# A decode kernel's w_up split between all partitions and the lower 64, and its output row stored by one engine

## The chip, the cores and the metric

The kernel runs on one core of one Trainium2 chip. The metric is the device time of one execution in microseconds (us), the median of several runs. A profile of one execution gives the trace; its span, from the program's first instruction to its last, is a little shorter than the device time.

## What is computed

One token is decoded by two branches that a scalar gate mixes. Branch A is attention of 32 query heads over the last 4096 positions of 8 key/value heads; branch B is a gated linear unit. The change touches only how `B_w_up` is loaded and multiplied and how the 512 outputs are stored.

```python
# x: 1x1x512, wq: 512x4096, caches: 1x8x65536x128, wo: 4096x512
# w_gate, w_up: 512x1792, w_down: 1792x512, gate_w: 512, all bf16
def reference(A_x, A_k_cache, A_v_cache, A_wq, A_wo, B_x, B_w_gate, B_w_up, B_w_down, gate_w):
    x = A_x
    g = sigmoid((x * gate_w).sum(-1, keepdims=True))
    q = x @ A_wq                                   # 32 heads of 128
    k, v = last 4096 positions of the caches       # each used by 4 query heads
    a = softmax(q @ k.T * 128**-0.5) @ v @ A_wo
    b = (sigmoid(x @ B_w_gate) * (x @ B_w_up)) @ B_w_down
    return g * a + (1 - g) * b                     # 1x1x512
```

## The kernel before

The work is mostly loading: 30.67 MB of weights and cache pass through once. SyncE issues the loads in this order: `wq_sb`, four `kn` (K), `wg_sb` (w_gate), `wu_sb` and two `wx_sb` (w_up), four `vv` (V), two `wo_sb`, four `wd_sb` (w_down). ScalarE loads only `x` and `gate_w`. `P` is 128, `D` 512, `DC` 4, `F` 1792, `FQ` 448 and `NJ` 14.

w_up stands in two tiles. Its first 384 rows lie in `wu_sb`, three rows to each of 128 partitions. Its last 128 rows lie in `wx_sb`, two rows to each of partitions 0 to 63, loaded 32 partitions at a time:

```python
    wg_sb = w14.tile([P, DC, F], BF16, name="wg_sb", tag="w14")
    dq.dma_start(wg_sb[:], B_w_gate.rearrange("(p c) f -> p c f", c=DC))
    wu_sb = w14.tile([P, DC, F], BF16, name="wu_sb", tag="w14")


    UC = DC - 1
    UR = UC * P
    dq.dma_start(wu_sb[:, 0:UC, :], B_w_up[0:UR, :].rearrange("(p c) f -> p c f", c=UC))
    wx_sb = const.tile([64, 2, F], BF16, name="wx_sb")
    wx_v = B_w_up[UR:D, :].rearrange("(b j i r) f -> b i j (r f)", b=2, j=4, i=8)
    for b in range(2):
        dq.dma_start(wx_sb[32 * b:32 * b + 32, :, :].rearrange("p r f -> p (r f)"), wx_v[b])
    # ...
    vv = []
    for a in range(HP):
        vv.append(blk.tile([P, NP, P], BF16, name="vv", tag="blk"))
        load_pair(vv[a], A_v_cache, a)
```

`vv` uses the same four buffers as `kn` (pool `blk`), so each `vv` load waits until VectorE has transposed the K tile before it.

The token `x` is turned into columns to match those layouts: four columns for rows `4p+c`, three for rows `3p+c`, and two columns of 64 for `wx_sb`:

```python
    xt_ps = ps_m.tile([P, DC + UC], F32, name="xt_ps", tag="m")
    for c in range(DC):
        nc.tensor.matmul(xt_ps[:, c:c + 1], lhsT=xr[:, 0, c:D:DC], rhs=ident[0:1, 0:1],
                         start=True, stop=True, skip_group_check=True)
    for c in range(UC):
        nc.tensor.matmul(xt_ps[:, DC + c:DC + c + 1], lhsT=xr[:, 0, c:UR:UC], rhs=ident[0:1, 0:1],
                         start=True, stop=True, skip_group_check=True)
    xx_ps = ps_m.tile([64, 2], F32, name="xx_ps", tag="m")
    xp = const.tile([1, 2, 64], BF16, name="xp")
    for r in range(2):
        nc.vector.tensor_copy(xp[:, r, :].rearrange("o (b i j) -> o b i j", b=2, j=4),
                              xr[:, 0, UR:D].rearrange("o (b j i r) -> o b i j r", b=2, j=4, i=8)[:, :, :, :, r])
        nc.tensor.matmul(xx_ps[:, r:r + 1], lhsT=xp[:, r, :], rhs=ident[0:1, 0:1],
                         start=True, stop=True, skip_group_check=True)
    xT = const.tile([P, DC + UC], BF16, name="xT")
    nc.vector.tensor_copy(xT[:], xt_ps[:])
    xx = const.tile([64, 2], BF16, name="xx")
    nc.vector.tensor_copy(xx[:], xx_ps[:])
```

The products of w_gate and w_up go to one PSUM tile each, four blocks of 448 columns on four groups of 32 partitions. `glu(1, ...)` stands after the attention product and takes (3 + 2) x 4 = 20 matmuls:

```python
    def glu(w, parts):
        for n, (x_c, w_c) in enumerate(parts):
            for j in range(4):
                nc.tensor.matmul(gu_ps[w][32 * j:32 * j + 32, 0:FQ], lhsT=x_c.to_broadcast([x_c.shape[0], 32]),
                                 rhs=w_c[:, j * FQ:(j + 1) * FQ], start=(n == 0), stop=(n == len(parts) - 1))
    # ...
    glu(1, [(xT[:, DC + c:DC + c + 1], wu_sb[:, c, :]) for c in range(UC)]
        + [(xx[:, r:r + 1], wx_sb[:, r, :]) for r in range(2)])
```

The end sums both branches in PSUM, the two halves of the row on partitions 0 and 32, then copies and stores each half. SyncE stores what VectorE copied, ScalarE what it copied itself:

```python
    for c in range(NC_O):
        add_row(oY[:, c:c + 1], wo_sb[:, c, :], c == 0, False)
    for j in range(NJ):
        add_row(hT[:, j, 0:1], wd_sb[:, j, :], False, j == NJ - 1)
    res = work.tile([P, HN], BF16, name="res")
    nc.vector.tensor_copy(res[0:1, :], a_ps[0:1, 0, 0:HN])
    nc.sync.dma_start(out[0, :, 0:HN], res[0:1, :])
    nc.scalar.copy(res[32:33, :], a_ps[32:33, 1, 0:HN])
    nc.scalar.dma_start(out[0, :, HN:N_OUT], res[32:33, :])
```

Of the kernel before, what the change touches and what calls it, by code (L numbers as in the profile page):

```python
# [12 lines left out]
BF16 = mybir.dt.bfloat16  # L13
F32 = mybir.dt.float32
# [3 lines left out]
def kernel(  # L18
# [14 lines left out]
    nc = tc.nc  # L33

    P = 128
    D = A_x.shape[-1]
    DC = D // P
# [8 lines left out]
    F = B_w_gate.shape[1]  # L46
    NJ = F // P
    N_OUT = A_wo.shape[1]
    NC_O = HQ * DH // P
    FQ = F // 4  # L50
# [11 lines left out]
    const = ctx.enter_context(tc.tile_pool(name="const", bufs=1))  # L62
# [4 lines left out]
    work = ctx.enter_context(tc.tile_pool(name="work", bufs=1))  # L67
    ps_big = ctx.enter_context(tc.tile_pool(name="ps_big", bufs=2, space=bass.MemoryType.PSUM))
    ps_S = ctx.enter_context(tc.tile_pool(name="ps_S", bufs=2, space=bass.MemoryType.PSUM))
    ps_m = ctx.enter_context(tc.tile_pool(name="ps_m", bufs=2, space=bass.MemoryType.PSUM))  # L70


    xr = const.tile([1, 2, D], BF16, name="xr")
# [3 lines left out]
    dq = nc.sync  # L77
# [15 lines left out]
    wg_sb = w14.tile([P, DC, F], BF16, name="wg_sb", tag="w14")  # L93
    dq.dma_start(wg_sb[:], B_w_gate.rearrange("(p c) f -> p c f", c=DC))
    wu_sb = w14.tile([P, DC, F], BF16, name="wu_sb", tag="w14")


    UC = DC - 1
    UR = UC * P
    dq.dma_start(wu_sb[:, 0:UC, :], B_w_up[0:UR, :].rearrange("(p c) f -> p c f", c=UC))  # L100
    wx_sb = const.tile([64, 2, F], BF16, name="wx_sb")
    wx_v = B_w_up[UR:D, :].rearrange("(b j i r) f -> b i j (r f)", b=2, j=4, i=8)
    for b in range(2):
        dq.dma_start(wx_sb[32 * b:32 * b + 32, :, :].rearrange("p r f -> p (r f)"), wx_v[b])

    vv = []
    for a in range(HP):
# [16 lines left out]
    ident = const.tile([P, P], BF16, name="ident")  # L124
# [17 lines left out]
    nc.vector.tensor_reduce(selI[:], identf[:].rearrange("p (x r) -> p r x", x=4), axis=AX.X, op=ALU.add)  # L142


    xt_ps = ps_m.tile([P, DC + UC], F32, name="xt_ps", tag="m")
    for c in range(DC):
        nc.tensor.matmul(xt_ps[:, c:c + 1], lhsT=xr[:, 0, c:D:DC], rhs=ident[0:1, 0:1],  # L147
                         start=True, stop=True, skip_group_check=True)
    for c in range(UC):
        nc.tensor.matmul(xt_ps[:, DC + c:DC + c + 1], lhsT=xr[:, 0, c:UR:UC], rhs=ident[0:1, 0:1],  # L150
                         start=True, stop=True, skip_group_check=True)
    xx_ps = ps_m.tile([64, 2], F32, name="xx_ps", tag="m")
    xp = const.tile([1, 2, 64], BF16, name="xp")
    for r in range(2):
        nc.vector.tensor_copy(xp[:, r, :].rearrange("o (b i j) -> o b i j", b=2, j=4),
                              xr[:, 0, UR:D].rearrange("o (b j i r) -> o b i j r", b=2, j=4, i=8)[:, :, :, :, r])
        nc.tensor.matmul(xx_ps[:, r:r + 1], lhsT=xp[:, r, :], rhs=ident[0:1, 0:1],
                         start=True, stop=True, skip_group_check=True)
    xT = const.tile([P, DC + UC], BF16, name="xT")
    nc.vector.tensor_copy(xT[:], xt_ps[:])  # L160
    xx = const.tile([64, 2], BF16, name="xx")
    nc.vector.tensor_copy(xx[:], xx_ps[:])
# [20 lines left out]
    for u in range(4):  # L183
        nc.tensor.matmul(S_ps[u // 2][:, u % 2, :], lhsT=other[:].rearrange("p o y u -> p (o y u)"),  # L184
                         rhs=ident[0:2, 0:2].rearrange("p (o y) -> p o y", o=1).to_broadcast([2, 256, 2]),
                         start=True, stop=False)
# [11 lines left out]
    for k in range(8):  # L198
        q_ps = ps_big.tile([P, 512], F32, name="q_ps", tag="b")
        ks = slice(k * 512, (k + 1) * 512)  # L200
        for c in range(DC):
            nc.tensor.matmul(q_ps[:], lhsT=xT[:, c:c + 1].to_broadcast([P, P]),  # L202
                             rhs=wq_sb[:, c, ks], start=(c == 0), stop=(c == DC - 1))
# [18 lines left out]
    for a in range(HP):  # L222
        for v in range(2):
            kT = kTs[a, v] if (a, v) in kTs else k_transpose(a, v)
            k_v = kT[:].rearrange("p (n dhi s t) -> p n dhi s t", n=KB, dhi=2, s=32)
            for dhi in range(2):
                for t in range(2):
                    for hb in range(2):
                        nc.tensor.matmul(S_ps[v][:, hb, :], lhsT=q_st[:, a, dhi, :, t],  # L229
                                         rhs=k_v[:, hb * 16:(hb + 1) * 16, dhi, :, t],  # L230
                                         start=False, stop=(a == HP - 1 and dhi == 1 and t == 1))


    gu_ps = [ps_big.tile([P, 512], F32, name="gu_ps", tag="b") for _ in range(2)]

    def glu(w, parts):
        for n, (x_c, w_c) in enumerate(parts):
            for j in range(4):
                nc.tensor.matmul(gu_ps[w][32 * j:32 * j + 32, 0:FQ], lhsT=x_c.to_broadcast([x_c.shape[0], 32]),  # L239
                                 rhs=w_c[:, j * FQ:(j + 1) * FQ], start=(n == 0), stop=(n == len(parts) - 1))  # L240


    pm2 = work.tile([P, 2], F32, name="pm2")
    for v in range(2):
        nc.vector.tensor_reduce(pm2[:, v:v + 1], S_ps[v][:].rearrange("p a b -> p (a b)"), axis=AX.X, op=ALU.max)  # L245
    pm = work.tile([P, 1], F32, name="pm")
    nc.vector.tensor_tensor(pm[:], pm2[:, 0:1], pm2[:, 1:2], op=ALU.max)
    glu(0, [(xT[:, c:c + 1], wg_sb[:, c, :]) for c in range(DC)])
    sge = work.tile([P, FQ], F32, name="sge")
    nc.scalar.activation(sge[:], gu_ps[0][:, 0:FQ], AF.Exp, scale=-1.0)  # L250
    mt_ps = ps_m.tile([1, P], F32, name="mt_ps", tag="m")
# [6 lines left out]
                     start=True, stop=True)  # L258
# [21 lines left out]
    HN = N_OUT // 2  # L280
    pv_ps = ps_S.tile([P, 4, P], F32, name="pv_ps", tag="S")
    a_ps = ps_S.tile([P, 2, 512], F32, name="a_ps", tag="S")

    def add_row(lhsT, rhs, start, stop):
        for i in range(2):
            nc.tensor.matmul(a_ps[32 * i:32 * i + 1, i, 0:HN], lhsT=lhsT, rhs=rhs[:, i * HN:(i + 1) * HN],  # L286
                             start=start, stop=stop)
# [5 lines left out]
    for a in range(HP):  # L293
        for m in range(NP // 4):
            nc.tensor.matmul(pv_ps[32 * a:32 * a + 32, :, :],  # L295
                             lhsT=eT[:, a, 4 * m:4 * m + 4, :].rearrange("p n r -> p (n r)"),
                             rhs=vv[a][:, 4 * m:4 * m + 4, :],
                             start=(m == 0), stop=(m == NP // 4 - 1))
# [6 lines left out]
    nc.scalar.copy(pv_sb[:], pv_ps[:])  # L305


    glu(1, [(xT[:, DC + c:DC + c + 1], wu_sb[:, c, :]) for c in range(UC)]
        + [(xx[:, r:r + 1], wx_sb[:, r, :]) for r in range(2)])

    o_ps = ps_m.tile([P, HQ], F32, name="o_ps", tag="m")
    for n in range(4):
# [21 lines left out]
        add_row(oY[:, c:c + 1], wo_sb[:, c, :], c == 0, False)  # L334
    for j in range(NJ):
        add_row(hT[:, j, 0:1], wd_sb[:, j, :], False, j == NJ - 1)
    res = work.tile([P, HN], BF16, name="res")
    nc.vector.tensor_copy(res[0:1, :], a_ps[0:1, 0, 0:HN])  # L338
    nc.sync.dma_start(out[0, :, 0:HN], res[0:1, :])
    nc.scalar.copy(res[32:33, :], a_ps[32:33, 1, 0:HN])  # L340
    nc.scalar.dma_start(out[0, :, HN:N_OUT], res[32:33, :])


# [28 lines left out]
```

## Time and profile before

| What | Value |
|---|---|
| Device time, median of 3 runs | 80.81 us (80.67 to 80.82) |
| Span of the profiled execution | 79.3 us |
| Read from HBM | 30.67 MB, 387 GB/s over the span |
| TensorE matmul busy | 52.9 us (67%) |
| VectorE busy | 38.8 us (49%) |
| ScalarE busy | 10.9 us (14%) |
| w_up loads | one of 1344 KB, two of 224 KB |
| Output stores | two of 0.5 KB |

How to read it: the profile page gives each engine's busy share, a row of forty digits that cuts the span into equal slices (a 9 is nine tenths or more busy), and a chain of work that is followed back from the last instruction: at each step to what released it. In the chain a load counts from its issue to its landing, so a load that waits long in its queue has a large share there. A busy share is an average over the span, and an engine's idle time matters only where the chain passes through it. The trace also holds a record for each DMA packet (start, length, bytes) and for each update of a semaphore; the last of these are how one sees when a load has landed on each of the DMA engines.

### The profile page before, as it was taken

The numbers are of one execution on the slowest core, as the hardware profiler recorded it, in microseconds if no ns is written. First come the engines' busy times: TensorE is split into PE (matmuls) and PEld (weight loads), VectorE is DVE, ScalarE is ACT, GpSimd is POOL, SyncE is SP. The second block draws the span as 40 slices with busy tenths as digits, with TensorE's granted clock in tenths as the row PEclk, the third lists the DMA queues.
The fourth block names the chain that finished last, engine by engine and source line by source line (L and its number), as shares of the span: only waits on it lengthen the run. The fifth ranks groups of instructions, "written<-read, shape, count | busy, mean of one in ns | idle before, by whom it ended". The sixth has DMA issues, their size and how long they took to land.

```text
span 79.3 us, 806 instructions
## 1 busy us (share of the span) xinstructions
PE 52.9 (67%) x318; PEld 24.0 (30%) x318; DVE 38.8 (49%) x52; ACT 10.9 (14%) x20; POOL 3.3 (4%) x10
## 2 busy tenths in 40 slices
PE   0200095999708788888896109999996799557650
PEld 0200041344203333333331103334541345346420
DVE  1600820039889999999956279923000000690020
ACT  2400000256740000000002470000000002000010
POOL 7900000000000000000000000000000000000000
PEclk9999999999999999999999975559999999999999
DMA  6779899999999999999999999999999999999600
GB/s 182 281 330 529 364 430 397 421 421 463 413 421 421 463 413 418 434 412 413 432 436 413 421 454 421 421 413 463 421 413 421 446 438 413 409 385 393 232 11 1
DMA packets 2538, 30.71 MB, mean 387 GB/s; under 512 B 292, under 2 KB 424, under 8 KB 744
## 3 DMA queue, kind: packets, MB, share of 16 engines
q1 hardware_dynamic: 2530, 30.67, 92.1%
q8 instruction: 2, 0.03, 0.2%
q10 hardware_dynamic: 6, 0.00, 0.0%
HBM read 30.67 MB, written 0.00 MB: 387 GB/s over the span
## 4 chain that ended last, share of the span: by engine, by line
DMA 78%; PE 11%; DVE 6%; ACT 1%; issue 0%
DMA wd_sb<-in_B_w_down_dram 36%; DMA vv<-in_A_v_cache_dram 26%; DMA wq_sb<-in_A_wq_dram 15%; PE q_ps L202 11%; DVE kT L190 3%; DVE qbig L218 2%; DVE qtT L207 1%; PE a_ps L286 1%; ACT q_sb L204 1%; DVE res L338 1%
## 5 line engine op out<-in xcount | busy, mean ns | idle before, releaser
L295 PE MATMUL pv_ps<-vv,eT 128*32 128x512 bf16 x64 | 16.7, 433 | 4.1 <-DVE eT L267 2.8
L229 PE MATMUL S_ps<-kT,qbig 128*128 128x512 bf16 x64 | 15.2, 378 | 5.0 <-DVE qbig L218 2.8
L190 DVE STREAM_TRANSPOSE kT<-kn 128x2048 f32<-128x2048 f32 x8 | 17.8, 2282 | 0.4 <-DMA kn<-in_A_k_cache_dram 0.3
L295 PEld LDWEIGHTS <-eT 128*32 128x32 bf16 x64 | 6.5, 108 | 13.3 <-issue 5.6
L229 PEld LDWEIGHTS <-qbig 128*128 128x128 bf16 x64 | 6.1, 97 | 14.1 <-issue 4.2
L202 PE MATMUL q_ps<-wq_sb,xT 128*128 128x512 bf16 x32 | 8.4, 427 | 1.0 <-DMA wq_sb<-in_A_wq_dram 1.0
L315 DVE TENSOR_TENSOR oT<-o_ps,rb 128x32 bf16<-128x32 f32 x1 | 0.2, 192 | 12.8 <-PE o_ps L313 12.8
L184 PE MATMUL S_ps<-ident,other 2*128 2x512 bf16 x4 | 2.0, 610 | 5.9 <-DVE other L139 5.9
L207 DVE STREAM_TRANSPOSE qtT<-q_sb 128x512 f32<-128x512 f32 x4 | 2.7, 690 | 6.0 <-ACT q_sb L204 6.0
L204 ACT CAST q_sb<-q_ps 128x512 bf16<-128x512 f32 x8 | 4.7, 586 | 6.4 <-PE q_ps L202 6.4
L202 PEld LDWEIGHTS <-xT 128*128 128x128 bf16 x32 | 3.4, 108 | 6.3 <-issue 3.5
L286 PE MATMUL a_ps<-wo_sb,oY 128*1 128x256 bf16 x64 | 3.8, 272 | 1.5 <-DMA wo_sb<-in_A_wo_dram 1.2
L286 PEld LDWEIGHTS <-oY 128*1 128x1 bf16 x64 | 2.7, 83 | 3.1 <-issue 1.4
L267 DVE STREAM_TRANSPOSE eT<-e_sb 128x1024 bf16<-128x1024 bf16 x2 | 2.4, 1224 | 1.9 <-ACT e_sb L265 1.9
L250 ACT ACTIVATE sge<-gu_ps 128x448 f32<-128x448 f32 x1 | 0.5, 544 | 18.9 <-PE gu_ps L239 18.9
L305 ACT COPY pv_sb<-pv_ps 128x512 f32<-128x512 f32 x1 | 0.6, 586 | 18.5 <-PE pv_ps L295 18.5
L167 DVE TENSOR_TENSOR gpr<-xr 1x512 f32<-1x512 bf16 x1 | 0.7, 679 | 4.8 <-DMA xr<-in_gate_w_dram 4.8
L277 DVE RECIPROCAL sg<-sge 128x448 f32<-128x448 f32 x1 | 3.0, 2953 | 0.0
L338 DVE CAST res<-a_ps 1x256 bf16<-1x256 f32 x1 | 0.4, 412 | 5.2 <-PE a_ps L286 5.2
L245 DVE TENSOR_REDUCE pm<-S_ps 128x1 f32<-128x1024 f32 x2 | 2.4, 1207 | 0.9 <-PE S_ps L229 0.9
L147 PE MATMUL xt_ps<-ident,xr 1*128 1x1 bf16 x4 | 0.3, 165 | 3.5 <-POOL ident L125 3.5
L286 PE MATMUL a_ps<-wd_sb,hT 128*1 128x256 bf16 x28 | 2.1, 271 | 0.8 <-DMA wd_sb<-in_B_w_down_dram 0.8
(64 smaller groups left out, 31.3 us busy)
## 6 DMA issues: line engine op xcount, KB each, us to landing
kn<-in_A_k_cache_dram SPq DMA_DIRECT2D x4, 2048.0 KB, 18.8
vv<-in_A_v_cache_dram SPq DMA_DIRECT2D x4, 2048.0 KB, 21.0
wq_sb<-in_A_wq_dram SPq DMA_DIRECT2D x1, 4096.0 KB
wo_sb<-in_A_wo_dram SPq DMA_DIRECT2D x2, 2048.0 KB, 26.6
wg_sb<-in_B_w_gate_dram SPq DMA_DIRECT2D x1, 1792.0 KB, 33.1
wu_sb<-in_B_w_up_dram SPq DMA_DIRECT2D x1, 1344.0 KB
wd_sb<-in_B_w_down_dram SPq DMA_DIRECT2D x1, 1024.0 KB
wx_sb<-in_B_w_up_dram SPq DMA_DIRECT2D x2, 224.0 KB
```

The lines of the kernel that those rows point to most:

```text
L184: nc.tensor.matmul(S_ps[u // 2][:, u % 2, :], lhsT=other[:].rearrange("p o y u -> p (o y u)"), rhs=ident[0:2, 0:2].rearrange("p (o y) -> p ...
L190: nc.vector.transpose(t[:].bitcast(F32), kn[a][:, v * KB:(v + 1) * KB, :] .rearrange("p n d -> p (n d)").bitcast(F32))
L202: nc.tensor.matmul(q_ps[:], lhsT=xT[:, c:c + 1].to_broadcast([P, P]), rhs=wq_sb[:, c, ks], start=(c == 0), stop=(c == DC - 1))
L204: nc.scalar.copy(q_sb[:, ks], q_ps[:])
L207: nc.vector.transpose(qtT[:].bitcast(F32)[:, kq], q_sb[:].bitcast(F32)[:, kq])
L218: copy(q_dst[rows, :, 32 * qd:32 * qd + R2, :, t], q_src[rows, :, :, :, 0, t])
L229: nc.tensor.matmul(S_ps[v][:, hb, :], lhsT=q_st[:, a, dhi, :, t], rhs=k_v[:, hb * 16:(hb + 1) * 16, dhi, :, t], start=False, stop=(a == HP ...
L245: nc.vector.tensor_reduce(pm2[:, v:v + 1], S_ps[v][:].rearrange("p a b -> p (a b)"), axis=AX.X, op=ALU.max)
L267: nc.vector.transpose(eT[:, :, v * KB:(v + 1) * KB, :].rearrange("p a n r -> p n a r"), e_sb[:, v, :].rearrange("p (n a r) -> p n a r", a= ...
L277: nc.vector.reciprocal(sg[:], sge[:])
L286: nc.tensor.matmul(a_ps[32 * i:32 * i + 1, i, 0:HN], lhsT=lhsT, rhs=rhs[:, i * HN:(i + 1) * HN], start=start, stop=stop)
L295: nc.tensor.matmul(pv_ps[32 * a:32 * a + 32, :, :], lhsT=eT[:, a, 4 * m:4 * m + 4, :].rearrange("p n r -> p (n r)"), rhs=vv[a][:, 4 * m:4 ...
```

## The change

w_up is cut differently. Now every partition p holds rows 4p to 4p+3, as w_gate does, except for the last three quarters (1344 columns) of row 4p+3. Those are kept aside in `wx_sb` on partitions 0 to 63: two halves of 64 rows side by side, in four loads of 32 partitions. So the part that goes only to the lower 64 partitions shrinks from 128 whole rows (458,752 bytes) to three quarters of 128 rows (344,064 bytes), and the part that goes to all partitions grows by the same 114,688 bytes. The purpose is to set the balance between what the lower half of the partitions gets and what the upper half gets. The columns of `x` for rows `3p+c` fall away, since w_up uses w_gate's; `glu` takes 4 + 4 + 4 + 1 + 3 x 2 = 19 matmuls for w_up.

At the end both copies write into one row on partition 0, and ScalarE stores all 512 values with one transfer; SyncE stores nothing. The purpose is to end the program with one store.

```diff
--- before.py
+++ after.py
@@ -94,14 +94,15 @@
     dq.dma_start(wg_sb[:], B_w_gate.rearrange("(p c) f -> p c f", c=DC))
     wu_sb = w14.tile([P, DC, F], BF16, name="wu_sb", tag="w14")
 
-
-    UC = DC - 1
-    UR = UC * P
-    dq.dma_start(wu_sb[:, 0:UC, :], B_w_up[0:UR, :].rearrange("(p c) f -> p c f", c=UC))
-    wx_sb = const.tile([64, 2, F], BF16, name="wx_sb")
-    wx_v = B_w_up[UR:D, :].rearrange("(b j i r) f -> b i j (r f)", b=2, j=4, i=8)
-    for b in range(2):
-        dq.dma_start(wx_sb[32 * b:32 * b + 32, :, :].rearrange("p r f -> p (r f)"), wx_v[b])
+    FX = 3 * FQ
+    LM = DC * F - FX
+    dq.dma_start(wu_sb[:].rearrange("p c f -> p (c f)")[:, 0:LM],
+                 B_w_up.rearrange("(p c) f -> p (c f)", c=DC)[:, 0:LM])
+    wx_sb = const.tile([64, 2, FX], BF16, name="wx_sb")
+    wx_v = B_w_up.rearrange("(h b j i c) f -> h b i j c f", h=2, b=2, j=4, i=8)[:, :, :, :, DC - 1, F - FX:F]
+    for h in range(2):
+        for b in range(2):
+            dq.dma_start(wx_sb[32 * b:32 * b + 32, h, :], wx_v[h, b])
 
     vv = []
     for a in range(HP):
@@ -142,21 +143,18 @@
     nc.vector.tensor_reduce(selI[:], identf[:].rearrange("p (x r) -> p r x", x=4), axis=AX.X, op=ALU.add)
 
 
-    xt_ps = ps_m.tile([P, DC + UC], F32, name="xt_ps", tag="m")
+    xt_ps = ps_m.tile([P, DC], F32, name="xt_ps", tag="m")
     for c in range(DC):
         nc.tensor.matmul(xt_ps[:, c:c + 1], lhsT=xr[:, 0, c:D:DC], rhs=ident[0:1, 0:1],
                          start=True, stop=True, skip_group_check=True)
-    for c in range(UC):
-        nc.tensor.matmul(xt_ps[:, DC + c:DC + c + 1], lhsT=xr[:, 0, c:UR:UC], rhs=ident[0:1, 0:1],
-                         start=True, stop=True, skip_group_check=True)
     xx_ps = ps_m.tile([64, 2], F32, name="xx_ps", tag="m")
     xp = const.tile([1, 2, 64], BF16, name="xp")
-    for r in range(2):
-        nc.vector.tensor_copy(xp[:, r, :].rearrange("o (b i j) -> o b i j", b=2, j=4),
-                              xr[:, 0, UR:D].rearrange("o (b j i r) -> o b i j r", b=2, j=4, i=8)[:, :, :, :, r])
-        nc.tensor.matmul(xx_ps[:, r:r + 1], lhsT=xp[:, r, :], rhs=ident[0:1, 0:1],
+    for h in range(2):
+        nc.vector.tensor_copy(xp[:, h, :].rearrange("o (b i j) -> o b i j", b=2, j=4),
+                              xr[:, 0, :].rearrange("o (h b j i c) -> o h b i j c", h=2, b=2, j=4, i=8)[:, h, :, :, :, DC - 1])
+        nc.tensor.matmul(xx_ps[:, h:h + 1], lhsT=xp[:, h, :], rhs=ident[0:1, 0:1],
                          start=True, stop=True, skip_group_check=True)
-    xT = const.tile([P, DC + UC], BF16, name="xT")
+    xT = const.tile([P, DC], BF16, name="xT")
     nc.vector.tensor_copy(xT[:], xt_ps[:])
     xx = const.tile([64, 2], BF16, name="xx")
     nc.vector.tensor_copy(xx[:], xx_ps[:])
@@ -233,11 +231,17 @@
 
     gu_ps = [ps_big.tile([P, 512], F32, name="gu_ps", tag="b") for _ in range(2)]
 
-    def glu(w, parts):
-        for n, (x_c, w_c) in enumerate(parts):
+    def glu(w, wsb):
+        for c in range(DC):
             for j in range(4):
-                nc.tensor.matmul(gu_ps[w][32 * j:32 * j + 32, 0:FQ], lhsT=x_c.to_broadcast([x_c.shape[0], 32]),
-                                 rhs=w_c[:, j * FQ:(j + 1) * FQ], start=(n == 0), stop=(n == len(parts) - 1))
+                g_out = gu_ps[w][32 * j:32 * j + 32, 0:FQ]
+                if w == 1 and c == DC - 1 and j >= 1:
+                    for h in range(2):
+                        nc.tensor.matmul(g_out, lhsT=xx[:, h:h + 1].to_broadcast([64, 32]),
+                                         rhs=wx_sb[:, h, (j - 1) * FQ:j * FQ], start=False, stop=(h == 1))
+                    continue
+                nc.tensor.matmul(g_out, lhsT=xT[:, c:c + 1].to_broadcast([P, 32]),
+                                 rhs=wsb[:, c, j * FQ:(j + 1) * FQ], start=(c == 0), stop=(c == DC - 1))
 
 
     pm2 = work.tile([P, 2], F32, name="pm2")
@@ -245,7 +249,7 @@
         nc.vector.tensor_reduce(pm2[:, v:v + 1], S_ps[v][:].rearrange("p a b -> p (a b)"), axis=AX.X, op=ALU.max)
     pm = work.tile([P, 1], F32, name="pm")
     nc.vector.tensor_tensor(pm[:], pm2[:, 0:1], pm2[:, 1:2], op=ALU.max)
-    glu(0, [(xT[:, c:c + 1], wg_sb[:, c, :]) for c in range(DC)])
+    glu(0, wg_sb)
     sge = work.tile([P, FQ], F32, name="sge")
     nc.scalar.activation(sge[:], gu_ps[0][:, 0:FQ], AF.Exp, scale=-1.0)
     mt_ps = ps_m.tile([1, P], F32, name="mt_ps", tag="m")
@@ -305,8 +309,7 @@
     nc.scalar.copy(pv_sb[:], pv_ps[:])
 
 
-    glu(1, [(xT[:, DC + c:DC + c + 1], wu_sb[:, c, :]) for c in range(UC)]
-        + [(xx[:, r:r + 1], wx_sb[:, r, :]) for r in range(2)])
+    glu(1, wu_sb)
 
     o_ps = ps_m.tile([P, HQ], F32, name="o_ps", tag="m")
     for n in range(4):
@@ -334,11 +337,10 @@
         add_row(oY[:, c:c + 1], wo_sb[:, c, :], c == 0, False)
     for j in range(NJ):
         add_row(hT[:, j, 0:1], wd_sb[:, j, :], False, j == NJ - 1)
-    res = work.tile([P, HN], BF16, name="res")
-    nc.vector.tensor_copy(res[0:1, :], a_ps[0:1, 0, 0:HN])
-    nc.sync.dma_start(out[0, :, 0:HN], res[0:1, :])
-    nc.scalar.copy(res[32:33, :], a_ps[32:33, 1, 0:HN])
-    nc.scalar.dma_start(out[0, :, HN:N_OUT], res[32:33, :])
+    res = work.tile([1, N_OUT], BF16, name="res")
+    nc.vector.tensor_copy(res[:, 0:HN], a_ps[0:1, 0, 0:HN])
+    nc.scalar.copy(res[:, HN:N_OUT], a_ps[32:33, 1, 0:HN])
+    nc.scalar.dma_start(out[0, :, :], res[:])
 
 
 # ---- launch: one core; inputs and outputs as the reference has them ----
```

## The prediction

> **What bounds the kernel now.** I read three views in this order: the page's DMA row and chain, then the chain in order of time, then the DMA view cut to the last microseconds. The page says that the load queue hardly pauses and that the end is a load:
>
> ```profile
> DMA  6779899999999999999999999999999999999600
> q1 hardware_dynamic: 2530, 30.67, 92.1%
> DMA 78%; PE 11%; DVE 6%; ACT 1%; issue 0%
> ```
>
> From the fourth slice to the 37th the 16 DMA engines are at nine tenths or more, so every engine's work must be read as hidden behind the stream until shown otherwise. The tail of the chain in order of time (start, length, what) is this:
>
> ```profile
> 47.28 28.65 DMA wd_sb<-in_B_w_down_dram
> 75.93 0.04 issue
> 75.97 0.66 PE a_ps L286 x6
> 76.63 0.40 DVE res L338
> ```
>
> The last six matmuls wait for the last pieces of w_down. So two things set the end: when the slowest DMA engine has worked off its queue, and the path from there to the stored row. The DMA view cut to 71 to 77 us (40 slices of 0.15 us) shows the first of them:
>
> ```profile
> DMA  9989897979999796755666565655421000000000
> GB/s 457 403 341 471 362 492 307 533 294 423 369 464 369 287 437 239 300 225 205 273 246 266 225 259 219 246 205 178 150 75 61 14 0 0 0 0 0 0 0 0
> ```
>
> At about 73.5 us the share falls from 9 tenths to 5 or 6 and stays there for 2 us: some engines are done, the others carry on alone at about 240 GB/s. The stream ends **unevenly**. The trace's semaphore updates say who is late. [...]The 16 updates of the last w_down piece come as six at 73.55 to 73.93, two at 75.41 and 75.50, and eight at 75.74 to 76.27. Before the w_up loads all 16 engines were together: w_gate's updates span 36.37 to 36.92. So the unevenness is made by what stands between.
>
> The end after the stream, by the timeline:
>
> ```profile
> 76.62 0.41 DVE L338 CAST res<-a_ps 1x256 bf16<-1x256 f32 x1 [5.21 <-PE a_ps L286]
> 76.65 0.36 ACT L340 CAST res<-a_ps 1x256 bf16<-1x256 f32 x1 [10.41 <-PE a_ps L286]
> 77.04 0.23 ACTq L341 DMA_DIRECT2D out_dram<-res  x1
> 77.06 0.28 SPq L339 DMA_DIRECT2D out_dram<-res  x1
> ```
>
> Two half rows are stored by two queues. By the semaphore updates ScalarE's store lands at 78.11 and SyncE's at 78.29; then the closing barrier runs to 79.3.
>
> [...]For the 32-partition loads of wx_sb the source's slowest dimension is 8. The trace agrees: each wx_sb load has eight late updates (40.74 to 41.25 and 41.82 to 42.35) and one early one (14.22 and 15.02). [...]The trace names no engines; I call the eight **low** and the others **high**. [...]The trace shows two packets of kind instruction with 16384 bytes, at 36.73 us (1061 ns) and 68.31 us (1099 ns). After each, one more high engine is about 1.5 us behind its fellows (w_up: 41.58 against at most 40.18 for the other 15). These are the two updates at 75.41 and 75.50.
>
> **The change part by part.** Costs come from the trace's packet records, one packet to a partition's run (median times): 2048 bytes 85 ns, 3072 bytes 125 ns, 7168 bytes 272 ns, 10752 bytes 407 ns, 14336 bytes 539 ns. They follow each other without gaps: a 2 MB vv load is 8 packets of 614 ns an engine, 4.91 us, and vv lands 4.90 us apart (47.26, 52.16).
>
> - *w_up's part for the low engines.* Removed: two loads of 32 partitions, 4 packets an engine each, 8 x 272 ns = 2.18 us. Added: four loads of 32 partitions with 1344 values, 16 packets of 2688 bytes an engine. Interpolated between 2048 and 3072 bytes, 85 + 40 x 640/1024 = 110 ns each, so 16 x 110 = 1.76 us. Low engines: -0.42 us.
> - *w_up's part for all engines.* A partition's run grows from 10752 to 11648 bytes. The slope is (539 - 407)/3584 = 0.037 ns a byte, so 896 bytes cost 33 ns; 8 packets an engine make +0.26 us on every engine.
> - *Sum.* Low: -0.42 + 0.26 = **-0.16 us**, last update 76.27 to about 76.11. High engines that had an instruction fetch: 75.50 + 0.26 = 75.76. The low ones still end last, so the stream ends about 0.15 us earlier. The change narrows the gap between the two groups from 2.18 to 1.76 us, close to the 1.5 us of one fetch; total bytes stay equal.
> - *The store.* Removed: SyncE's store, which landed last. Added: ScalarE's store waits for VectorE's copy too (77.03 against 77.01) and carries 1 KB instead of 512 B (46 ns against 28 ns a packet). Before, it took 1.07 us from issue to landing. One more wait may cost some 0.03 us. That gives 77.07 + 1.07 + 0.02 = 78.16 against 78.29, so -0.13 us, and SyncE has one semaphore fewer to look at after it (the last wait ended 0.06 us after the store's). I take **-0.15 us**.
> - *TensorE and VectorE.* Three single-column matmuls go at the start, and w_up takes 19 matmuls instead of 20. None is on the path: at the start TensorE waits for wq_sb until 13.0 us, and after w_up it idles 1.24 us for wo_sb at 71.83. Worth 0.
> - *Issue order.* Two more loads stand in SyncE's queue, and the eight load semaphores go round by two places. The first vv load then also waits for the third K load rather than the first, the next for the fourth, then for w_gate and for w_up.
>
> Together: 80.81 - 0.16 - 0.15 = 80.50 us.
>
> **The rivals.** First, *the vv loads come too late*. SyncE's waits before are
>
> ```profile
> SPq L84 <- DVE kT L190: 19.8, 4, 8.6
> SPq L104 <- DMA wq_sb<-in_A_wq_dram: 8.0, 1, 8.0
> ```
>
> that is, the vv loads are held by the buffers that VectorE's transposes free (first at 26.53 us). Afterwards the first waits for the third K load, which landed at 27.73, and the last for w_up, some 41.9 instead of 39.69. But the queue then still holds K, w_gate and w_up up to about 42 us, and the last vv load is wanted only near 57 us. I expect later issues and no hole. A hole would add its own length.
>
> Second, *short packets cost more than I interpolate*, because a run now begins 896 bytes into a row. At 150 ns the low engines would take 16 x 150 = 2.40 us, 0.22 more than before, plus 0.26: the time would be about 81.2. The w_down pieces, also strided runs, stand at 85 and 125 ns without such a loss, so I hold this unlikely.
>
> Third, *the fetch lands elsewhere*. The instruction stream is a little shorter. If one of the fetches fell to a low engine, its 1.5 us would come on top of the longest queue: about +1.4 us, 81.9. Both fell to high engines before and the count of blocks should not change, so one in twenty. If the high engines became the last, the gain of 0.16 would shrink, not turn round.
>
> Fourth, *the one store gains nothing*. [...]here a 28 ns packet takes 1.07 us to land. If the 0.18 us between the two landings is scatter, the store gives 0 and the time is 80.65.
>
> **Range and chances.** The middle is 80.50. Either gain missing puts it at 80.65; both a little larger at 80.25. The runs of before spread over 0.15 us. Dear short packets or a misplaced fetch stretch the upper side. So 80.2 to 80.9 eight times in ten. Two per cent is 1.6 us, which no part of the sum reaches: faster 0.01, same 0.97, slower 0.02.
>
> **What would show it.** In the changed profile: wx_sb's last update stands about 1.76 us after w_up's on the low engines, packets of 2688 bytes near 110 ns; w_down's last landing is 0.15 us earlier; the low plateau in the cut DMA view is shorter; one store, issued by ScalarE at about 0.45 us after the last matmul; the DMA row stays at 9 around 42 us. Wrong would be: a slice under 9 in the middle (rival one), packets well over 110 ns (two), a last group of other make-up (three), or the same time from last matmul to end (four).

## The result, and the profile after

The changed kernel takes 80.42 us (median of 6 runs, 80.33 to 80.65) against 80.81 us. The ratio is 0.9956, with a 95% interval of 0.9935 to 0.9976: a gain of 0.36 us, well under 2%. A second comparison (e5, below) gave 0.9956 again (0.9940 to 0.9971). The forecast was 80.50 us in a range of 80.2 to 80.9. Some executions (two of four in e10) take 1.2 to 1.9 us longer than the rest of the same kernel; the times leave them out, and the profiles of e2 and e6 come from such executions, so their last landings are not compared with the others'.

The page of the changed kernel, its DMA row, its load queue and its chain:

```profile
DMA  7779799999999999999999999999999999999710
q1 hardware_dynamic: 2608, 30.67, 92.9%
DMA 93%; SPq 2%; PE 1%; DVE 1%; issue 0%
```

The same bytes go through the same queue in 78 packets more (2608 against 2530), and no slice from the sixth to the 37th falls under 9. The chain has lost TensorE's part, which looks like a large change and is none: it now runs back through a V load that waited for a K load, not for a transpose. Both are waits in SyncE's queue far ahead of the need.

The tail of its chain in order of time (start, length, what):

```profile
46.84 28.67 DMA wd_sb<-in_B_w_down_dram
75.51 0.04 issue
75.55 0.66 PE a_ps L290 x6
76.20 0.40 DVE res L341
```

Its DMA view cut to 71 to 77 us, as before (40 slices of 0.15 us):

```profile
DMA  9999796969899979986666665664100000000000
GB/s 382 437 382 403 321 492 253 580 273 471 355 457 369 423 273 389 416 307 266 246 246 246 246 232 219 239 212 157 48 0 0 0 0 0 0 0 0 0 0 0
```

The four tail pieces have the same lengths as before, to 0.02 us, and stand 0.42 to 0.44 us earlier. The plateau at 6 tenths is still there, but shorter, and it ends in a cliff instead of a stair (6 6 4 1, where it was 5 5 4 2 1). The 16 updates of the last w_down piece read: six at 74.06 to 74.29, ten at 75.52 to 75.84. That each update stands for one engine is my reading, and the DMA share fits it: from 74.2 to 75.2 us, with ten updates to come, it is 0.61 of the 16 engines (10/16 is 0.63). By the same reading the ten are the two that are late after an instruction packet and the eight low ones, and they now end together.

The end, by the timeline:

```profile
76.20 0.41 DVE L341 CAST res<-a_ps 1x256 bf16<-1x256 f32 x1 [5.23 <-PE a_ps L290]
76.23 0.36 ACT L342 CAST res<-a_ps 1x256 bf16<-1x256 f32 x1 [10.42 <-PE a_ps L290]
76.68 0.23 ACTq L343 DMA_DIRECT2D out_dram<-res  x1
```

The one store lands at 77.77 us, 1.57 us after the first copy began; the later of the two stores landed 1.67 us after it.

### The profile page after: what moved, and what is told of

Its sections match the earlier page's. It is cut to its first block, busy times and chain, and to the rows that moved or that the text cites. A ratio compares the mean times of both kernels' runs of the same rounds, so it can differ in the third digit from the quotient of the medians.

```text
span 78.7 us, 798 instructions
## 1 busy us (share of the span) xinstructions
PE 52.5 (67%) x314; PEld 23.6 (30%) x314; DVE 38.8 (49%) x52; ACT 10.9 (14%) x20; POOL 3.3 (4%) x10
## 3 DMA queue, kind: packets, MB, share of 16 engines
q1 hardware_dynamic: 2608, 30.67, 92.9%
## 4 chain that ended last, share of the span: by engine, by line
DMA 93%; SPq 2%; PE 1%; DVE 1%; issue 0%
DMA wd_sb<-in_B_w_down_dram 36%; DMA kn<-in_A_k_cache_dram 32%; DMA vv<-in_A_v_cache_dram 24%; SPq L84 2%; PE a_ps L290 1%; DVE res L341 1%; SPq L80 0%
## 5 line engine op out<-in xcount | busy, mean ns | idle before, releaser
L299 PE MATMUL pv_ps<-vv,eT 128*32 128x512 bf16 x64 | 15.9, 405 | 4.1 <-DVE eT L271 2.8
```

The lines of the kernel that those rows point to most:

```text
L299: nc.tensor.matmul(pv_ps[32 * a:32 * a + 32, :, :], lhsT=eT[:, a, 4 * m:4 * m + 4, :].rearrange("p n r -> p (n r)"), rhs=vv[a][:, 4 * m:4 ...
```

## The experiments

Times are medians; every ratio is to the kernel before, run on the same chip.

### Each part alone (e1, e2), and both again (e5)

The new w_up with the old end:

```diff
-    res = work.tile([1, N_OUT], BF16, name="res")
-    nc.scalar.dma_start(out[0, :, :], res[:])
+    res = work.tile([P, HN], BF16, name="res")
+    nc.sync.dma_start(out[0, :, 0:HN], res[0:1, :])
+    nc.scalar.dma_start(out[0, :, HN:N_OUT], res[32:33, :])
```

> The new w_up split with the old two stores. Theory (the stream ends with its slowest DMA engine, and the new split takes 0.16 to 0.27 us from the eight low ones): 80.55 to 80.65 us, last w_down landing about 0.25 us earlier than before, ten late updates of the last w_down piece of which eight are the low engines. Rival (the split does nothing, all the gain is the single store): 80.8 us. SyncE's store lands about 0.18 us after ScalarE's again.

Measured: 80.66 us, ratio 0.9985 (0.9975 to 0.9995). The last w_down piece lands at 76.11 us against 76.27, 0.16 us earlier and not 0.25; ten of its updates are late (75.49 to 76.11), as expected. SyncE's store lands 0.17 us after ScalarE's (78.13, 77.96). The split gains by itself, but little: the ratio is worth 0.12 us, and the time stands just above what was expected.

The old w_up with the new end (the same edit the other way round):

> The old w_up split with the new single store. Theory (the store is worth 0.15 us): 80.65 us; from the start of the last copy to the landing of the store about 1.57 us instead of 1.67, and from there to the end 0.97 instead of 1.03. Rival (the split does nothing): 80.4 us, the whole gain. Second rival (the 0.18 us between the two landings was scatter): 80.8 us.

Measured: 80.71 us, ratio 0.9986 (0.9977 to 0.9996). The store gains by itself, so neither rival stands, though both intervals, this one and e1's, end just short of 1. From the start of the first copy to the landing it takes 1.58 us, as expected; from there to the end it takes 1.10 us and not 0.97.

The changed kernel once more, unedited:

> The changed kernel again, beside the kernel before on the same chip as the single parts' neighbours. If the two parts simply add (ratios 0.9985 and 0.9986): ratio 0.997, 80.55 us. If they help each other: 0.995 or less.

Measured: 80.44 us, ratio 0.9956 (0.9940 to 0.9971). It ran on another chip than e1 and e2. The single gains add to 0.0029, the pair has 0.0044. The intervals overlap, so this may be scatter. The traces show a second reason, though it was not tested by itself: at the end SyncE looks at the DMA semaphores one after another, 0.06 to 0.07 us each where nothing is left to land (77.39 and 77.46, 78.31 and 78.37 us in the kernel before). The program's loads and stores take eight semaphores in turn, so here the number of loads decides how many looks come after that at the store's. From the last store's landing to the end of the span it takes 1.03 us in the kernel before, where one more look follows, 1.09 us in e1 and 1.10 us in e2, where two follow, and 0.97 and 0.99 us in the changed kernel and e5, whose store happens to use the last semaphore. So each part alone pays one look more than the kernel before, and the pair one look less: together three looks, by my estimate (three times 0.06 us) some 0.18 us or 0.0022, which is enough for the difference of 0.0015. That is luck of the pair.

### The amount on the low engines, or the layout? (e8)

```diff
-    FX = 3 * FQ
+    FX = F
```

`glu` takes all four blocks of the last row from `wx_sb` accordingly. So 128 whole rows stand on the lower partitions, as in the kernel before, but in the changed kernel's four loads.

> The changed kernel with the whole of every fourth row of w_up on the lower partitions (FX = F): the old amount, 128 rows, in the new layout of four loads with one row a packet. Theory (the amount on the low engines sets the end): 16 packets of 3584 bytes at about 140 ns make 2.24 us against 2.18 before, so as the old split with the single store, or up to 0.1 us slower: 80.7 to 80.8 us. Rival (the layout of rows or four loads instead of two make the gain): 80.45 us.

Measured: 80.69 us, ratio 0.9984 (0.9973 to 0.9995), the ratio of the single store alone. From the mean update of w_gate to the mean update of the last wx_sb load there are 5.40 us here, 5.40 in the kernel before, and 5.16, 5.17, 5.14 and 5.09 in the changed kernel, e1, e5 and e9. So the gain in the stream is the **amount** on the low engines, and its size is 0.24 us in the changed kernel's profile (0.23 to 0.31 in the four).

### No extra on the low engines (e4)

```diff
-    dq.dma_start(wu_sb[:].rearrange("p c f -> p (c f)")[:, 0:LM], ...)
-    for h in range(2):
-        for b in range(2):
-            dq.dma_start(wx_sb[32 * b:32 * b + 32, h, :], wx_v[h, b])
+    dq.dma_start(wu_sb[:], B_w_up.rearrange("(p c) f -> p c f", c=DC))
```

`xx` and its columns of `x` fall away, and `glu` takes all of w_up from `wu_sb`.

> The changed kernel without wx_sb: w_up is loaded like w_gate, 14336 bytes to each of 128 partitions, in one load. Theory (the extra on the low engines fills the time of an instruction fetch on the others): high engines 8 x (539 - 446) = 0.74 us later, low ones 0.97 us earlier; the last updates are those of the engines with a fetch, 0.4 us later than the last of the changed kernel: 80.85 us, level with the kernel before less its store. Rival (fewer, longer packets are simply better): 80.3 us or less.

Measured: 81.13 us, ratio 1.0037 (1.0023 to 1.0052). The last piece's updates: fourteen at 74.50 to 74.89 and two at 76.19 and 76.48, the last 0.64 us after the changed kernel's. The form is as expected, the size somewhat larger. Fewer and longer packets do not help: the DMA row cut to 71 to 78 us stands at 1 tenth from 74.3 to 75.7 us (2/16 is 0.13), so two engines work on alone, and they set the time.

### Sixteen engines for the same bytes (e3): the forecast that failed

```diff
-    wx_v = B_w_up.rearrange("(h b j i c) f -> h b i j c f", h=2, b=2, j=4, i=8)[...]
+    wx_v = B_w_up.rearrange("(h b j i c) f -> h b i j c f", h=2, b=2, j=2, i=16)[...]
```

The columns of `x` are reordered in the same way.

> The changed kernel, but the same bytes and packets of wx_sb laid over partitions so that the source's slowest dimension is 16 instead of 8. Theory (that dimension sets how many engines a load uses): 16 late updates for each wx_sb load, no low group left; every high engine gets 0.86 us more and every low one 0.86 us less, so the last w_down piece comes as 14 updates close together and one or two about 1.5 us later, from engines that fetched instructions; last landing 0.5 us later than in the changed kernel, 80.95 us. Rival (only the total of bytes counts): as the changed kernel, 80.4 us.

Measured: 82.29 us, ratio 1.0185 (1.0172 to 1.0198). Every wx_sb load has 16 late updates, where those of the changed kernel have eight: the number followed the source's slowest dimension (16 against 8). The last piece shows fourteen updates together and two late, as expected too. But the fourteen come at 75.72 to 76.25 and the two at 77.33 and 77.55, about a microsecond later than I had worked out. The packets tell most of it: 2688 bytes take 200 ns (median), where they take 107 ns in the changed kernel. In the stage view from 40 to 41 us the last two numbers are DMA share and GB/s; a packet counts whole where it starts, so a share can exceed 1. First the changed kernel:

```profile
40.00:41.00 1.00, 0.95 (x5) 0.46 (x5) 1.00 (x1) 0.00 (x0) 0.00 (x0) 1.00 1.05 417
```

Then e3:

```profile
40.00:41.00 1.00, 0.78 (x4) 0.26 (x3) 1.00 (x2) 0.00 (x0) 0.00 (x0) 1.00 1.40 284
```

The engines are no less busy and move a third less. Twice as many engines, counted by the late updates, wrote to 32 partitions at a time. As an estimate from the packets, each engine spent 8 x 200 ns = 1.6 us, which is what the low ones alone had needed (1.62 us, by the landings in the changed kernel): the high engines gained work and the low ones lost hardly any. Against the 0.86 us an engine that I had counted this is 0.74 us more; the rest was not traced to a cause.

### Where the bytes land (e6, e7)

The loads as in the changed kernel, on 8 engines, but into partitions 64 to 127:

```diff
-            dq.dma_start(wx_sb[32 * b:32 * b + 32, h, :], wx_v[h, b])
+            dq.dma_start(wx_sb[64 + 32 * b:64 + 32 * b + 32, h, :], wx_v[h, b])
```

`xx` and its matmuls move to partitions 64 to 127 as well.

> The changed kernel with wx_sb on partitions 64 to 127 instead of 0 to 63; loads, engines used (source's slowest dimension 8) and bytes are the same. Theory A (only the number of bytes on each DMA engine counts): nothing changes, 80.4 us, packets of 2688 bytes at 107 ns. Theory B ([...]which made the 16-engine run's packets take 200 ns): [...]packets of 2688 bytes take about 200 ns, low and high engines both lose about 1.7 us, 82.1 us.

Measured: 82.16 us (two runs), ratio 1.0166 (1.0129 to 1.0203), 1.7 us over the changed kernel. Packets of 2688 bytes take 209 ns (median), and V's packets beside them up to 1.27 us instead of 0.61. Theory A is out: with bytes and the source's slowest dimension (8) alike, the partitions they are written to cost 1.7 us. Nor are wx_sb's packets alone longer, for V's grew too. That fits theory B, a rate shared by the engines that write to the same partitions, with 209 ns for its 200. But no trace names an engine or a partition, so who else writes to partitions 64 to 127 was assumed and not shown.

And on all 128 partitions, 16 engines, one load of short packets:

```diff
-    wx_sb = const.tile([64, 2, FX], BF16, name="wx_sb")
+    wx_sb = const.tile([P, FX], BF16, name="wx_sb")
+    dq.dma_start(wx_sb[:], B_w_up.rearrange("(p c) f -> p c f", c=DC)[:, DC - 1, F - FX:F])
```

`glu` multiplies them with w_gate's columns of `x`, and `xx` falls away.

> The changed kernel with wx_sb's 1344 columns on all 128 partitions in one load of 2688 bytes to a partition. Theory B (sharing of partitions' write side made the 16-engine run slow): [...]packets take 107 ns, 8 x (446 + 107 - 539) = 0.11 us more an engine than one whole load, so 81.2 us, 0.1 over the kernel without wx_sb. Rival (short packets are slow whenever all 16 engines run them): 200 ns a packet, about 82 us.

Measured: 81.31 us, ratio 1.0051 (1.0032 to 1.0069); packets at 107 ns. Short packets on 16 engines are not slow in themselves. What differs in e3 is that its 16 engines wrote to 32 partitions at a time and not to 128 (200 ns against 107). That fits theory B too; how the engines are spread over the partitions no run shows.

### Which engine issues the one store (e9)

```diff
-    nc.scalar.dma_start(out[0, :, :], res[:])
+    nc.sync.dma_start(out[0, :, :], res[:])
```

> The changed kernel with its one store issued by SyncE instead of ScalarE. If the later of the two old stores was late because SyncE's stores take longer (1.23 us from issue to landing against 1.07): landing 0.16 us later than in the changed kernel, ratio to the kernel before about 0.9975. If it was late because it was the second of two: same as the changed kernel, ratio 0.9956.

Measured: 80.53 us, ratio 0.9961 (0.9947 to 0.9976). SyncE's only store lands 1.12 us after its issue, ScalarE's only store 1.09 us after. With two stores SyncE's took 1.23. The ratio's interval reaches both expectations, so the landings decide: SyncE's store was late for being one of two (1.23 us against 1.12), and the choice of ScalarE is worth some 0.03 us in these two profiles.

### Who the late high engines are (e10)

```diff
+    pad_ps = ps_m.tile([1, 1], F32, name="pad_ps", tag="m")
+    for _ in range(128):
+        nc.tensor.matmul(pad_ps[:], lhsT=ident[0:1, 0:1], rhs=ident[0:1, 0:1], ...)
     xT = const.tile([P, DC], BF16, name="xT")
```

> The changed kernel with 128 single-element matmuls more at the start, while TensorE waits for wq_sb[...]. If the late high engines are those that fetch TensorE's instructions: three packets of kind instruction with 16384 bytes in the span instead of two, and one more engine late by 1.5 us, so five early updates in the last w_down piece instead of six (or one of the late ones later still, if one engine fetched twice); time as the changed kernel, 80.45 us, unless a fetch falls to an engine that is late already (then about 81.6 us). If the late engines have another cause: six early updates as before, whatever the fetches do.

Measured: 80.51 us (median of two runs, no interval). There are three packets of 16384 bytes of kind instruction, at 16.08, 42.96 and 70.24 us. Right after the first, one of the 16 updates of the first K load comes at 19.19 us, the others at 17.49 to 17.92. The DMA row cut to 71 to 78 us, first of the changed kernel:

```profile
DMA  8996989999897998565666641000000000000000
```

Then of e10:

```profile
DMA  9997989999897998767776662000000000000000
```

The plateau lies higher by about one engine of 16 (7 tenths instead of 6), and the updates are five at 74.09 to 74.39 and eleven at 75.62 to 76.03. With 128 matmuls and 128 weight loads more (442 of each against 314) there is one fetch more, three against two, and one engine more that is late: the late high engines are those that fetched TensorE's instructions.

## Why the prediction was right, point by point

- **What bounds the kernel** held. In all twelve profiles the first copy starts 0.35 us after the last w_down update, whatever the split was. The gain and every loss in the stream go through that update. (One reading was off without harm: the DMA row of before stands at nine tenths from the sixth slice, not from the fourth; the fifth has an 8.)
- **w_up's part for the low engines** had the right sign and was sized short: net -0.16 forecast, -0.24 measured (5.40 to 5.16 us). The term that was off is the packet of 2688 bytes. I interpolated 110 ns; it takes 107, and the four loads, each of four packets an engine, land only 0.41 us apart (40.57, 40.99, 41.39, 41.79 in mean landings), so 16 packets cost 1.62 us and not 1.76. Of the 0.24 us, e1's time shows 0.12 (its interval is 0.04 to 0.20), for the reasons given at e5 and under the last landing.
- **w_up's part for all engines** held nearly: 11648 bytes take 446 ns against my 440, so 8 packets add 0.31 us and not 0.26. The two errors partly cancel.
- **The order of the ends** held barely, if at all: I expected the slowest low engine 0.35 us after the fetching ones. After the split the first fetching engine lands w_up at 41.77 us and the slowest low one its last wx_sb piece at 41.92, 0.15 us later; before these were 41.58 and 42.35. Which of the ten late updates of w_down belongs to which group the trace does not tell.
- **The last landing** moved 0.43 us in the profile and not 0.16. Only 0.24 of it is the split. The rest is the slowest low engine, which stood 0.30 us behind the mean of the eight in the profile of before (42.35 against 42.05) and 0.13 in that of after (41.92 against 41.79). In e1 and e5, with the same split, it stood 0.35 and 0.23 us behind. One pair of profiles flatters the change; the ratio does not.
- **The store** held in size: -0.15 forecast, -0.16 in the two profiles. First copy to landing went from 1.67 to 1.57 us, in all ten profiles of kernels with one store (1.56 to 1.60), and the closing waits lost 0.06 us. But I counted that one look less to the store, and e2 has the single store and two looks after it: it came of the split's two added loads, which moved the store to the last semaphore. The other step, that ScalarE's second wait costs 0.03 us, shows as an issue 0.49 us after the first copy began instead of 0.43 us, so it costs 0.06.
- **The first rival**, late V loads, is what SyncE's waits now show:

```profile
SPq L84 <- DMA kn<-in_A_k_cache_dram: 8.4, 2, 4.2
SPq L84 <- DMA wu_sb<-in_B_w_up_dram: 4.3, 1, 4.3
SPq L84 <- DMA wg_sb<-in_B_w_gate_dram: 3.7, 1, 3.7
```

  The four V loads wait for K, w_gate and w_up instead of for VectorE, and the last is issued at 41.83 us instead of 39.69. The queue had no hole: 417 GB/s from 40 to 41 us, and V lands 4.91 us apart (4.90 before).
- **The second and fourth rivals** fell by the packet length and by e2. **The third** did not occur in the changed kernel's profile: both fetches stood on high engines. That was luck, and one in twenty looks too low: in two of the twelve profiles, e2's and e6's, both fetches fell on low engines. In e2 one of the eight updates of each wx_sb load comes 1.6 us after the last of the other seven (at 42.53 and 43.62 us), and the last w_down piece has eight updates at 73.57 to 73.97, six at 75.68 to 75.84 and two at 77.48 and 77.54, 1.7 us after the six.
- **A premise that was too narrow** did no harm here and cost 1.7 to 1.9 us in e3 and e6. I counted bytes on each engine only. Which partitions the low engines write in the other loads was my assumption and is not shown. e3 and e6 show that what counts as well is which partitions a load goes to and how many engines write there: packets of 2688 bytes took 200 and 209 ns, against 107 in the changed kernel.

## What to carry to other kernels

When loads are the bound, look at the updates of the last load's semaphore engine by engine: here the stream ended with its slowest engine, and a mean GB/s hid some 2 us in which only eight or ten of 16 engines worked (73.93 to 76.27 us in the kernel before). Bytes can be shifted to the engines that would be early, but look at the packets' times after it: with 107 ns the shift gained 0.24 us, while other engines (e3, 200 ns) or other partitions (e6, 209 ns) for the same bytes cost 1.7 to 1.9 us, more than the 0.7 us that no shift at all cost (e4, 81.13 us against 80.42). Read such gains in tenths of a microsecond from differences within one trace and from many runs, since the slowest engine's lag moved by 0.2 us from one profile to the next (0.13 to 0.35 us behind the mean in four).

## What the runs showed of the hardware that I had not expected

The time of a packet did not follow from its length alone. Packets of 2688 bytes took 107 ns where eight engines loaded 32 of partitions 0 to 63 at a time (changed kernel) and where 16 loaded all 128 (e7); they took 200 ns where 16 loaded 32 of partitions 0 to 63 at a time (e3) and 209 ns where the changed kernel's loads went to partitions 64 to 127 (e6). I read this as a rate shared by the engines that write to the same partitions; how many partitions would share one, and which engines write to them, no run shows.

And one refill of TensorE's instructions, a packet of about 1.1 us (1061 and 1104 ns in the changed kernel), holds one engine back: its update comes 1.5 to 1.9 us after the mean of the others in the first load after the packet (1.51 us in e10 after its first refill, 1.58 in the changed kernel, 1.69 in the kernel before, 1.85 in e7). It did not catch up: in the last w_down piece of the kernel before, the two stand at 75.41 and 75.50 us, 1.6 and 1.7 us after the mean of the first six (73.82). e10 added one by adding instructions.
